# Attention scores of consecutive head pairs on the two diagonals of the matmul array, in two PSUM banks

## The chip, the cores and the metric

The program runs on one core of a Trainium2 chip. The metric is the device time of one execution in microseconds (us), the median of several executions. The matmul engine is called TensorE or PE; its weight loads are listed apart as PEld. VectorE is DVE, ScalarE is ACT, GpSimd is POOL, and SP is the engine whose queue issues the DMAs.

## The reference

A sliding-window attention (2 batches, 8 heads, 576 positions, head size 64, window 64) feeds two mixture blocks. In the attention stage, cut to what matters:

```python
scores = (1 / np.sqrt(64)) * np.matmul(q, k.transpose(0, 1, 3, 2))
rel = pos[:, None] - pos[None, :]
scores = np.where((rel >= 0) & (rel < 64), scores, -1e9)
attn = softmax(scores)                  # over the last axis, + 1e-9 in the divisor
x = np.matmul(attn, v)                  # then laid out as 1152 tokens x 512
```

Then `x` goes through four dense experts, `out += p_e * (relu(x @ w1[e]) @ w2[e])` (512 to 1024 to 512), and the sum of those through `g = prelu(out @ w_in); g @ w_out` (512 to 2048 to 512). Everything is float32.

## The kernel before

The attention is cut into 18 blocks `j` of 64 queries. A block looks at 128 keys, its own 64 and the 64 before. The eight heads are handled as four pairs `hp` (`NP = 4`), each pair with one head `h` on partitions 0 to 63 and the other on 64 to 127. For a block there are these steps:

- `S` (`att_S`): eight source matmuls, one for each head, contracting 64 partitions into 64 query rows by 128 keys (line 222). Head `h` reads partition half `h` of `q` and `k` and writes partition half `h` of one PSUM bank, so that all eight use one diagonal of the array: upper rows with left columns, lower rows with right columns. A float32 matmul appears in the trace as two MATMULs with a weight load each, so a block has 16. Then DVE adds the mask and takes the row extreme, once for each pair (line 233), and ACT takes the exponentials and their sums, once for each pair (line 236).
- `N` (`att_N`): DVE turns the sums into reciprocals (lines 242, 243), POOL multiplies (line 244).
- `PT` (`att_PT`): four transposes on TensorE (line 250), copied out by DVE or ACT (lines 254, 256).
- `PV` (`att_PV`): eight source matmuls (16 in the trace) over all 128 rows with 64 columns, the two heads of a pair on the two column halves (line 267). The result is split into a high and a low part (`xhi`, `xlo`; lines 272 to 278).

The order is written out by hand. For step `j` it is `PT(j-3)`, `N(j-1)`, `S(j)`, `PV(j-4)` (a little different at the start), with extras: `W` splits a quarter of the first weights (a DVE cast to `w1h`, line 157, and a POOL subtraction to `w1l`, line 158), and `Q` loads the next queries (line 90) and, once, the keys of the second batch (line 93). Blocks 0 to 9 come ahead of the dense layers; blocks 10 to 17 are spread between units of the first expert stage, one unit being 12 matmuls (`l1_unit`, line 290, or `l2_products`, line 324). After that TensorE runs dense units to the end. Each engine runs its instructions in the order written; SP's queue issues the DMAs in that order too, and a weight load (line 115, two buffers `ws`) waits until the splits of the load two before are done. The third weight load, `w2` of the first stage, is ahead of the small loads `praw` and `alph`, the fourth `q` load and the second `k` load in SP's queue.

PSUM is one pool of eight one-bank buffers, taken in turn. A tile of any kind is one such buffer.

Of the kernel before, what the change touches and what calls it, by code (L numbers as in the profile page):

```python
# [16 lines left out]
P = 128  # L17
# [8 lines left out]
def tile_kernel(ctx, tc, q, k, v, probs, w1, w2, w_in, w_out, alpha, out):  # L26
    nc = tc.nc


    B, H, D, S = k.shape  # L30
    NP = H // 2
    NT, DM = out.shape
    E, _, F = w1.shape
# [23 lines left out]
    def psum(name):  # L57
        return pp.tile([P, 512], F32, tag="ps", name=name)
# [154 lines left out]
    def att_S(j):  # L213
        g, jb = divmod(j, GB)
        m = mask0 if j % NB == 0 else mask
        ps = psum(f"s{j}")
        sv = ps.rearrange("p (a k) -> p a k", a=NP)

        for hp in range(NP):
            for h in range(2):  # L220
                r = slice(D * h, D * h + D)
                nc.tensor.matmul(  # L222
                    sv[r, hp, :],
                    lhsT=qs[g % 3][r, hp, jb * BLK:(jb + 1) * BLK],
                    rhs=kts[j // NB][r, hp, (j % NB) * BLK:(j % NB) * BLK + P],
                    start=True, stop=True, skip_group_check=True,
                )

        sm = ab.tile([P, NP, P], F32, tag="sm", bufs=2, name=f"sm{j}")
        st = ab.tile([P, 4, NP], F32, tag="st", bufs=4, name=f"st{j}")  # L230
        pt = ab.tile([P, NP, P], F32, tag="p", bufs=4, name=f"p{j}")
        for hp in range(NP):
            nc.vector.tensor_tensor_reduce(out=sm[:, hp, :], in0=sv[:, hp, :], in1=m, scale=-(D ** -0.5), scalar=3.0e38,  # L233
                                           op0=ALU.add, op1=ALU.min, accum_out=st[:, 0, hp:hp + 1])
        for hp in range(NP):
            nc.scalar.activation(out=pt[:, hp, :], in_=sm[:, hp, :], func=AF.Exp, scale=-1.0,  # L236
                                 bias=st[:, 0, hp:hp + 1], accum_out=st[:, 1, hp:hp + 1])
        p_t[j] = (pt, st)
# [20 lines left out]
    def att_PV(j):  # L259
        t, vt = pt_t.pop(j), v_t[j]  # L260
        ps = psum(f"pv{j}")[:, 0:NP * BLK]
        pv = ps.rearrange("p (a t) -> p a t", a=NP)

        for hp in range(NP):
            tv = t[:, hp, :].rearrange("p (h t) -> p h t", h=2)
            for h in range(2):
                nc.tensor.matmul(pv[64 * h:64 * h + 64, hp, :], lhsT=vt[:, 2 * hp + h, :], rhs=tv[:, h, :],  # L267
                                 start=True, stop=True, skip_group_check=True)
        c, o = divmod(j * BLK, CH)
        hi, lo = xhi[c][:, :, o:o + BLK], xlo[c][:, :, o:o + BLK]  # L270
        if o + BLK == CH:
            nc.scalar.activation(out=hi, in_=pv, func=AF.Copy)
            nc.vector.tensor_tensor(out=lo, in0=pv, in1=hi.bitcast(F32), op=ALU.subtract)
        else:
            xf = ab.tile([P, NP, BLK], F32, tag="xf", bufs=2, name=f"xf{j}")
            nc.vector.tensor_copy(out=xf, in_=pv)
            nc.gpsimd.tensor_copy(out=hi, in_=xf)
            nc.gpsimd.tensor_tensor(out=lo, in0=xf, in1=hi.bitcast(F32), op=ALU.subtract)
# [84 lines left out]
    with tc.manual_schedule():  # L363
# [24 lines left out]
        for j in range(NBLK + 4):  # L388
            last = (j - 3) % (CH // BLK) == 0
            pv = [("PV", j - 4)] if 0 <= j - 4 < NBLK else []  # L390
# [20 lines left out]
        def att_step():  # L411
            if pos[0] >= len(steps):
                return
            op, j = steps[pos[0]]
            pos[0] += 1
            if op == "Q":
                load_q(j)
                if j == 3:
                    load_k(1, 0, S)
            elif op == "S":  # L420
                att_S(j)
            elif op == "N":
                att_N(j)
            elif op == "W":
                split_w((1, 0, j // 2), j, fast=True)
            elif op == "PT":
                att_PT(j)
            else:
                att_PV(j)
                if j + 6 < NBLK:  # L430
                    load_v(j + 6)
                done[0] = j + 1
# [21 lines left out]
        s, c = NST - 1, NCH - 1  # L454
# [9 lines left out]
        a, b = S1 - 1, S1  # L464
# [7 lines left out]
        for s in range(1, NST):  # L472
            p = s - 1
# [27 lines left out]
        for i, unit in enumerate(order):  # L501
            op, s, c, a = unit
# [64 lines left out]
```

## Time and profile before

| what | us |
| --- | --- |
| three runs | 665.4, 667.4, 667.59 (median 667.4) |
| profiled execution, its own time | 667.37 |
| its span, first to last instruction | 665.6 |
| TensorE busy | 648.3 (97%) |
| mean granted TensorE clock | 0.995 |

The span is 1.8 us shorter than the time of the same execution. Busy time of TensorE counts each matmul from its start until its modelled end, so matmuls that overlap count once, and a busy engine need not be at its peak.

### The profile page before, as it was taken

Reading aid. Unit: us, or ns where it says so; the run is one execution under the profiler, and the core shown is the slowest. Engines: PE = TensorE matmul, PEld = TensorE weight load, DVE = VectorE, ACT = ScalarE, POOL = GpSimd, SP = SyncE. Lnnn points to the kernel's source line nnn. Section 1 sums busy time; section 2 is a strip of 40 time slices with the busy share of each in tenths; the row PEclk is TensorE's granted clock in tenths of the full one; section 3 lists DMA queues with packets and bytes.
Section 4 is the critical chain, followed back from the end, with each engine's and each line's share of the span. In section 5 each row is a group of like instructions: output and inputs, shape, how many; then the busy total and the mean of one; then the engine's idle time right before and its main releaser. Section 6 shows DMA issues by size and latency. Waiting matters only on the chain.

```text
span 665.6 us, 9448 instructions
## 1 busy us (share of the span) xinstructions
PE 648.3 (97%) x3720; PEld 584.6 (88%) x3720; DVE 390.4 (59%) x754; ACT 226.0 (34%) x539; POOL 187.7 (28%) x182
## 2 busy tenths in 40 slices
PE   5799999999999999999999999999999999999998
PEld 5598889999999999999999999999999887999897
DVE  3765543333383383393393342878777878888622
ACT  4554421221131131131131121334555443444331
POOL 5924410000030030030030000334665546566421
PEclk9999999999999999999999999999999998999999
DMA  8844011101121121121112101112111101110011
GB/s 292 252 139 129 1 64 64 63 1 64 63 64 63 64 64 63 64 64 64 64 64 63 64 1 63 64 64 64 41 61 61 57 37 64 64 64 0 32 40 71
DMA packets 25003, 45.71 MB, mean 69 GB/s; under 512 B 4352, under 2 KB 6656, under 8 KB 24960
## 3 DMA queue, kind: packets, MB, share of 16 engines
q1 hardware_dynamic: 24960, 45.12, 20.3%
q8 instruction: 29, 0.48, 0.3%
q14 instruction: 14, 0.11, 0.1%
HBM read 42.76 MB, written 2.36 MB: 68 GB/s over the span
## 4 chain that ended last, share of the span: by engine, by line
PE 94%; DVE 2%; DMA 2%; POOL 1%; issue 0%; SPq 0%; POOLq 0%; DVEq 0%
PE o L324 44%; PE h L290 44%; PE s L222 2%; DMA kt<-in_k_dram 2%; PE pt L250 1%; PE pv L267 1%; PE x L357 1%; POOL p L244 0%; POOL hl L317 0%; DVE sm L233 0%; DVE acc L349 0%; DVE gg L310 0%; POOL cy L197 0%; DVE cr L183 0%; POOL w1l L158 0%
## 5 line engine op out<-in xcount | busy, mean ns | idle before, releaser
L324 PE MATMUL o<-w2h,hl 128*128 128x512 f32 (+1 forms) x436 | 170.8, 392 | 1.3 <-POOL hl L317 1.3
L324 PE MATMUL o<-w2l,hh 128*128 128x512 f32 (+1 forms) x436 | 170.3, 390 | 0.1
L324 PE MATMUL o<-w2h,hh 128*128 128x512 f32 (+1 forms) x436 | 170.0, 390 | 0.0
L197 POOL TENSOR_TENSOR cy<-cy,ce 128x512 f32<-128x512 f32 x32 | 47.1, 1470 | 361.7 <-DVE ce L189 361.7
L300 ACT ACTIVATE hh<-h 128x384 fp32r<-128x384 f32 x96 | 47.2, 492 | 238.4 <-PE h L290 238.1
L290 PE MATMUL h<-xhi,w1l 128*128 128x384 f32 x576 | 125.5, 339 | 0.0
L290 PE MATMUL h<-xlo,w1h 128*128 128x384 f32 x576 | 123.4, 335 | 0.0
L290 PE MATMUL h<-xhi,w1h 128*128 128x384 f32 x576 | 123.0, 334 | 0.0
L301 DVE SCALAR_TENSOR_TENSOR hl<-h,hh 128x384 fp32r<-128x384 f32 x96 | 53.5, 557 | 106.1 <-ACT hh L300 106.1
L290 PEld LDWEIGHTS h<-xhi,w1l 128*128 128x128 f32 x576 | 102.1, 189 | 3.0 <-DVE st L242 0.2
L290 PEld LDWEIGHTS h<-xlo,w1h 128*128 128x128 f32 x576 | 102.8, 188 | 0.0
L290 PEld LDWEIGHTS h<-xhi,w1h 128*128 128x128 f32 x576 | 101.9, 188 | 0.0
L324 PEld LDWEIGHTS o<-w2h,hl 128*128 128x128 f32 x436 | 82.2, 188 | 20.4 <-POOL hl L317 3.4
L324 PEld LDWEIGHTS o<-w2l,hh 128*128 128x128 f32 x436 | 82.3, 189 | 16.3 <-ACT hh L316 0.5
L324 PEld LDWEIGHTS o<-w2h,hh 128*128 128x128 f32 x436 | 82.3, 189 | 16.1
L345 DVE SCALAR_TENSOR_TENSOR acc<-o,pn,acc 128x512 f32<-128x512 f32 x63 | 46.6, 748 | 73.6 <-PE o L324 73.6
L317 POOL TENSOR_TENSOR hl<-gg,hh 128x384 fp32r<-128x384 f32 x48 | 53.1, 1116 | 59.5 <-ACT hh L316 57.4
L310 DVE SCALAR_TENSOR_TENSOR gg<-rn,alph,gg 128x384 f32<-128x384 f32 x48 | 39.8, 830 | 34.9 <-ACT gg L309 34.7
L236 ACT ACTIVATE p<-sm,st 128x128 f32<-128x128 f32 x72 | 28.1, 391 | 28.4 <-DVE st L233 28.4
L308 ACT ACTIVATE rn<-h 128x384 f32<-128x384 f32 x48 | 23.3, 486 | 31.5 <-PE h L290 31.2
L316 ACT ACTIVATE hh<-gg 128x384 fp32r<-128x384 f32 x48 | 25.2, 524 | 16.8 <-DVE gg L310 16.8
L222 PE MATMUL s<-kt,q 64*64 64x128 f32 x288 | 22.4, 305 | 7.8 <-DMA kt<-in_k_dram 7.8
(64 smaller groups left out, 565.5 us busy)
## 6 DMA issues: line engine op xcount, KB each, us to landing
ws<-in_moe_w_dram SPq DMA_DIRECT2D x15, 1024.0 KB, 5.2
ws<-in_moe_w_in_dram SPq DMA_DIRECT2D x8, 1024.0 KB, 5.2
ws<-in_moe_w_out_dram SPq DMA_DIRECT2D x8, 1024.0 KB, 5.0
v<-in_v_dram SPq DMA_DIRECT2D x16, 256.0 KB, 7.3
q<-in_q_dram SPq DMA_DIRECT2D x6, 384.0 KB, 6.9
out_dram<-acc SPq DMA_DIRECT2D x8, 256.0 KB, 2.0
kt<-in_k_dram SPq DMA_DIRECT2D x1, 1152.0 KB, 7.7
ws<-in_moe_w_dram SPq DMA_DIRECT2D x2, 512.0 KB, 8.3
```

The source lines that it names most:

```text
L197: nc.gpsimd.tensor_tensor(out=y, in0=y, in1=e.bitcast(F32), op=ALU.mult)
L222: nc.tensor.matmul(sv[r, hp, :], lhsT=qs[g % 3][r, hp, jb * BLK:(jb + 1) * BLK], rhs=kts[j // NB][r, hp, (j % NB) * BLK:(j % NB) * BLK + P ...
L236: nc.scalar.activation(out=pt[:, hp, :], in_=sm[:, hp, :], func=AF.Exp, scale=-1.0, bias=st[:, 0, hp:hp + 1], accum_out=st[:, 1, hp:hp + 1])
L290: nc.tensor.matmul(ps, lhsT=w[:, d * P:(d + 1) * P], rhs=x[:, d, :], start=(n == 0), stop=(n == 3 * KD - 1))
L300: nc.scalar.activation(out=hh, in_=ps, func=AF.Relu)
L301: nc.vector.scalar_tensor_tensor(out=hl, in0=ps, scalar=0.0, in1=hh.bitcast(F32), op0=ALU.max, op1=ALU.subtract)
L308: nc.scalar.activation(out=rn, in_=ps, func=AF.Relu, scale=-1.0)
L310: nc.vector.scalar_tensor_tensor(out=gg, in0=rn, scalar=alph[:, col:col + 1], in1=gg, op0=ALU.mult, op1=ALU.add)
L316: nc.scalar.activation(out=hh_, in_=gg_, func=AF.Copy)
L317: nc.gpsimd.tensor_tensor(out=hl_, in0=gg_, in1=hh_.bitcast(F32), op=ALU.subtract)
L324: nc.tensor.matmul(ps, lhsT=h_t[s, c, f][a][:, t * P:(t + 1) * P], rhs=w_t[2, s, f][b][:, cols], start=(n == 0), stop=(n == 3 * NF - 1))
L345: nc.vector.scalar_tensor_tensor(out=at, in0=ps, scalar=sc, in1=at, op0=ALU.mult, op1=ALU.add)
```

## The change

Pairs with an odd number swap the halves of the output: head 0 (upper rows) writes partitions 64 to 127, head 1 (lower rows) writes 0 to 63. They thus use the other diagonal of the array. The even pairs' scores stand in one PSUM tile, the odd pairs' in a second one, each of which is half filled. In `att_PV` the halves are read back accordingly. The number of matmuls, of DVE, ACT and POOL instructions, and of DMAs stays as it was.

```diff
     def att_S(j):
         g, jb = divmod(j, GB)
         m = mask0 if j % NB == 0 else mask
-        ps = psum(f"s{j}")
-        sv = ps.rearrange("p (a k) -> p a k", a=NP)
+
+        ps = [psum(f"s{j}_{i}")[:, 0:NP // 2 * P].rearrange("p (a k) -> p a k", k=P) for i in range(2)]
+        sv = [ps[hp % 2][:, hp // 2, :] for hp in range(NP)]
 
         for hp in range(NP):
             for h in range(2):
-                r = slice(D * h, D * h + D)
+                r, c = [slice(D * x, D * x + D) for x in (h, h ^ hp & 1)]
                 nc.tensor.matmul(
-                    sv[r, hp, :],
+                    sv[hp][c],
                     lhsT=qs[g % 3][r, hp, jb * BLK:(jb + 1) * BLK],
...
-            nc.vector.tensor_tensor_reduce(out=sm[:, hp, :], in0=sv[:, hp, :], in1=m, scale=-(D ** -0.5), scalar=3.0e38,
+            nc.vector.tensor_tensor_reduce(out=sm[:, hp, :], in0=sv[hp], in1=m, scale=-(D ** -0.5), scalar=3.0e38,
...
-                nc.tensor.matmul(pv[64 * h:64 * h + 64, hp, :], lhsT=vt[:, 2 * hp + h, :], rhs=tv[:, h, :],
+                nc.tensor.matmul(pv[64 * h:64 * h + 64, hp, :], lhsT=vt[:, 2 * hp + h, :], rhs=tv[:, h ^ hp & 1, :],
```

## Rows read from the trace of the kernel before

**Rows 1.** The page: busy time, and by slice TensorE's granted clock and DMA.

```profile
PE 648.3 (97%) x3720; PEld 584.6 (88%) x3720; DVE 390.4 (59%) x754; ACT 226.0 (34%) x539; POOL 187.7 (28%) x182
...
PE 94%; DVE 2%; DMA 2%; POOL 1%; issue 0%; SPq 0%; POOLq 0%; DVEq 0%
```

**Rows 2.** The chain that ended last, 36 to 95 us: start, length, what.

```profile
38.67 1.02 PE s L222 x16
39.69 0.61 PE pv L267 x16
40.30 0.59 PE pt L250 x4
40.89 2.09 PE h L290 x12
...
64.64 4.17 PE h L290 x24
```

**Rows 3.** Line 222, 33 to 80 us: durations in ns (min/median/max), starts.

```profile
L222 PEld LDWEIGHTS s<-kt,q x128: 129/133/133, 38.6 to 73.8; 64*64 64x64 f32 x128
L222 PE MATMUL s<-kt,q x128: 269/269/320, 38.6 to 74.0; 64*64 64x128 f32 x128
```

**Rows 4.** Line 222 in a tenth-us stretch: width, busy (instructions in flight), clock, DMA.

```profile
39.08:39.19 0.11, 0.11 (x6) 0.11 (x4) 1.00 0.05 19
```

**Rows 5.** The chain, 0 to 36 us.

```profile
5.83 3.69 PE s L222 x32
...
23.43 7.68 DMA kt<-in_k_dram
...
31.24 1.74 PE s L222 x16
32.98 1.04 PE pt L250 x4
```

**Rows 6.** The chain over the whole span, at the first dense units.

```profile
34.02 4.65 PE h L290 x24
```

**Rows 7.** DVE in order of time, 5 to 40 us.

```profile
7.97 0.29 DVE L233 CUSTOM_DVE_ANT_0 sm<-s,mask 128x128 f32<-128x128 f32 x1 [6.83 <-PE s L222]
...
12.38 0.40 DVE L157 CAST w1h<-ws 128x512 fp32r<-128x512 f32 x1
13.86 0.29 DVE L233 CUSTOM_DVE_ANT_0 sm<-s,mask 128x128 f32<-128x128 f32 x1 [1.08 <-PE s L222]
```

**Rows 8.** ACT in order of time, 8.3 to 13.6 us.

```profile
8.30 0.40 ACT L236 ACTIVATE p<-sm,st 128x128 f32<-128x128 f32 x1 [6.28 <-DVE st L233]
...
13.12 0.57 ACT L256 ACTIVATE ptr<-pt 128x512 f32<-128x512 f32 x1
```

**Rows 9.** POOL in order of time, 11 to 24 us.

```profile
11.04 1.04 POOL L244 TENSOR_TENSOR p<-p,st 128x512 f32<-128x512 f32 x1 [6.30 <-DVE st L243]
12.61 1.07 POOL L244 TENSOR_TENSOR p<-p,st 128x512 f32<-128x512 f32 x1 [0.53 <-DVE st L243]
13.63 1.27 POOL L158 TENSOR_TENSOR w1l<-ws,w1h 128x512 fp32r<-128x512 f32 x1
15.28 1.06 POOL L244 TENSOR_TENSOR p<-p,st 128x512 f32<-128x512 f32 x1 [0.38 <-DVE st L243]
16.31 1.27 POOL L158 TENSOR_TENSOR w1l<-ws,w1h 128x512 fp32r<-128x512 f32 x1
```

**Rows 10.** SP's queue in order of time.

```profile
17.61 0.38 SPq L115 DMA_DIRECT2D ws<-in_moe_w_dram  x1
```

**Rows 11.** The first weight load's landing after its issue at 3.90 us.

```profile
DMA to landing us min/median/max: 7.8/7.8/7.8
```

**Rows 12.** One stretch: width, busy PE, PEld, DVE, ACT, POOL, clock, DMA share, GB/s.

```profile
16.00:18.00 2.00, 1.63 (x22) 1.27 (x20) 1.97 (x13) 1.14 (x6) 2.00 (x3) 1.00 0.01 5
```

**Rows 13.** Stretches around the stop before 31 us, same columns.

```profile
28.10:31.50 3.40, 1.41 (x25) 1.13 (x27) 1.85 (x11) 2.39 (x10) 3.24 (x6) 1.00 1.05 404
31.60:34.90 3.30, 3.30 (x22) 2.97 (x19) 1.83 (x11) 1.49 (x8) 1.04 (x1) 0.50 1.05 327
```

## Prediction

> **What bounds the kernel now.** I read the page first: TensorE is busy 97% of the span and carries 94% of the chain that ended last [rows 1]. A change on TensorE can therefore count in full, but only where TensorE itself sets the pace. For that I read the chain in order of time. From 34 us on it is TensorE work almost without a break: a block's scores take 1.02 us on it, its values 0.61, its transposes 0.59, then 12 dense matmuls 2.09 [rows 2]. Eight of the 18 score blocks lie there: 128 MATMULs of line 222 between 38.6 and 74.0 us, 16 a block [rows 3]. Before 34 us the chain is mixed: scores, POOL, DVE, and a key load that is issued at 23.43 us and holds up block 9 until 31.24 us [rows 5].
>
> Next, what a block's 1.02 us is made of. Transposes and scores both stream 128 float32 columns. The transposes use the whole array one after the other: four in 0.59 us. Were the 16 scores also one after the other, they would need four times that less some start-up, at least 1.8 us. Say one slot is t and filling and draining the array cost D: 4t + D = 0.59 and 8t + D = 1.02 give t = 0.108 and D = 0.16 us. The value matmuls stream half as many columns: 8 x 0.054 + 0.16 = 0.59, against 0.61 in the row. So the trace says that two matmuls already run side by side in a slot, in the scores on the two quarters of one diagonal, in the values on the two column halves over all rows. The other diagonal lies idle during the scores.
>
> **The change, part by part.** The 16 MATMULs of a block stay, and so do all DVE, ACT, POOL and DMA instructions. Only the place of half of them in the array moves.
>
> Scores on the dense part of the chain. With four quarters at work a block has four slots: 4 x 0.108 + 0.16 = 0.59 us, 0.43 less than 1.02. What no row shows is two row halves writing the same 64 output partitions at once. The nearest rows bound it: the values show two column halves reading the same partitions together (gain as above); if the new pairing does not overlap at all, a block keeps eight slots (gain 0). In between, if the second diagonal starts one slot late, there are five slots and a gain of 0.32. I take 0.43, since nothing in the rows separates the two diagonals but the output partitions, and those now lie in two banks. Eight blocks: 3.44 us. TensorE waits for nothing else in this stretch, so I count it in full.
>
> Block 9 starts when the key load lands and takes 1.74 us, as its clock falls to half on the way [rows 5, 13]. It gains 0.43 at full and 0.85 at half clock. I take 0.6.
>
> The start. Blocks 0 and 1 take 3.69 us for 16 slots, 0.23 a slot, twice the later ones [rows 5]. DVE gets block 0 at 7.97 us [rows 7]. Four slots fewer bring that to 7.05, and ACT's first exponential from 8.30 to 7.4. ACT runs three blocks without a gap until 13.12, 1.61 each [rows 8]; it now ends them at 9.0, 10.6 and 12.2. Block 1's normalization no longer stands behind block 2's scores, and POOL's multiply goes from 12.61 to about 11.2 [rows 9], ending at 12.3. DVE's first weight cast at 12.38 [rows 7] may move to 11.75, as its load, issued at 3.90, has landed at 11.70 [rows 11]. POOL's first subtraction goes from 13.63 to 12.3, and DVE's row extremes of block 3 from 13.86 to 12.2, right behind the cast (TensorE has block 3 by then: POOL's first multiply at 9.7 instead of 11.04, transposes, four slots). POOL's third multiply then follows at 13.7 instead of 15.28 and its second subtraction at 14.8 instead of 16.31 [rows 7, 9]. That subtraction frees the buffer for the third weight load, which SP issues at 17.61 [rows 10]; now at about 16.1. Behind it in SP's queue stand the small loads, a query load and the key load. The DMA engines are idle in front of it, share 0.01 from 16 to 18 us [rows 12], so the whole train can move forward, and the key load lands about 1.5 us sooner, with block 9. Bounds: 0, if the train runs into the loads before it or the key load is held up on its way anyway, and 1.6. I take 1.4.
>
> PSUM. A block takes two buffers of the eight instead of one, so five instead of four are taken per step of about 4.3 us, and a buffer comes round after 1.6 steps, 7 us, instead of 2. Copies out follow within about 2 us, so this costs nothing; without that cover the first score matmul would wait for DVE. DVE can start a pair as soon as its bank is done, no later than now. Cost 0; upper bound one more wait instruction a block on TensorE's queue, below 0.05 us each, 0.4 over eight blocks.
>
> Here one rule speaks against the change. In the row, weight loads and matmuls of both row halves are in flight at any moment: in 0.11 us, six matmuls and four loads, both busy throughout [rows 4]. The Trainium skill, "TensorE: Matmul & The Clock Gate", Part 3 (what overlaps and what doesn't), says that a weight load overlaps matmuls in flight only when its row group differs. By that rule the present block could not load at all under its matmuls, so the trace disagrees, and the sum goes by the row.
>
> Sum: 3.44 + 0.6 + 1.4 = 5.4 us. The profiled execution took 667.37 us (span 665.6), as the median, 667.4. Its time becomes 662.0 us, its span 660.2.
>
> **The rivals.**
>
> *The start's gain is swallowed.* The key load takes 7.68 us from issue to landing [rows 5], with other loads beside it; if it lands as before, block 9 waits for it as before, and only 3.44 + 0.6 are left: 663.4 us. For it speaks the load's length, against it the idle DMA engines in front.
>
> *The diagonals don't overlap.* Two row halves on the same output partitions may take turns. Then a block keeps eight slots and nothing else changes: 667.4 us. The trace neither shows nor excludes this. A sentence on the page alone: the Trainium skill, "TensorEngine Tiling (Array Packing)", Gotcha 1, lets different row tiles work at once when they write different banks, which would give the four slots.
>
> *Slower: the weight loads come into the open.* If a load into one diagonal can't run while the other diagonal's matmuls hold the same rows, each of the four pairs of a block begins with its load, 0.133 us [rows 3], in front: 0.53 a block on top of eight slots. Eight blocks 4.3, block 9 0.5, and blocks 0 and 1 at half clock 8 x 0.23 = 1.8: 6.6 us, 674.0. It decides from 0.107 us a pair, where it eats the 0.43. Against it speaks rows 4, where loads run under matmuls of the same rows already; but there a quarter loads only for itself. The rule of the Trainium skill named above would give this case.
>
> *The clock.* After a stretch where TensorE was busy 1.41 of 3.40 us, the granted clock was 0.50, that is 1.2 of 2.4 GHz, for 31.6 to 34.9 us [rows 13]. It cost 0.72 in block 9, 0.45 in its transposes and 0.48 in the first 24 dense matmuls (4.65 against 4.17), 1.65 in all [rows 2, 5, 6]. Shorter scores leave TensorE idle longer in the start; the fall may come earlier and be over before block 9, or come once more. This is 1.65 either way and shifts each case.
>
> **How the numbers follow.** Four slots with the start's gain 0.55 (662.0), four or five slots without it 0.20 (663.4), no overlap 0.15 (667.4), loads in the open 0.10 (674.0). Own range of the first two: lowest 667.4 - (1.6 + 0.85 + 3.5 + 1.65) = 659.8; highest without the start's gain, with 0.43 for block 9, 3.0 for the others and a fall of the clock more, 667.4 - 1.8 = 665.6. That holds three in four; to eight in ten the range must reach the no-overlap case: 659.8 to 667.6. A measurement of this kernel can tell about 0.3%, 2.0 us, from no change. Faster by more 0.75, within 0.15, slower 0.10.
>
> **What would show it.** Right: line 222's 16 MATMULs in 0.59 us from block to next operation, eight matmuls or more in flight in a tenth of a us, the third weight load issued near 16.1 and block 9 started near 29.8 us, and everything from 90 us on shifted by one amount. Wrong: a block still at 1.02 us (no overlap) or above 1.1 (loads); block 9 still at 31.2 us (start swallowed); stops of TensorE on DVE in front of the scores (PSUM buffers); a second stretch at half clock.

## The result, and the profile after

The changed kernel takes 660.4 us (median of six runs, 660.15 to 663.17), the kernel before, on the same chip, 667.28 (665.4 to 667.59). The ratio is 0.991, with a 95% interval of 0.989 to 0.993. The forecast was 662.0.

The profiled execution took 660.32 us, its span is 658.5 against 665.6 before, so there are 7.1 us to find. The page of the changed kernel gives TensorE, with the same 3720 MATMULs, 8.4 us less busy time than [rows 1], and 92% of the chain instead of 94:

```profile
PE 639.9 (97%) x3720; PEld 574.3 (87%) x3720; DVE 390.7 (59%) x754; ACT 224.9 (34%) x539; POOL 187.9 (29%) x182
...
PE 92%; DVE 4%; DMA 2%; POOL 2%; issue 1%; ACT 0%; SPq 0%; POOLq 0%; DVEq 0%
```

The chain of the changed kernel, 36 to 95 us (start, length, what), answers to [rows 2]:

```profile
42.69 0.60 PE s L223 x16
43.28 0.61 PE pv L268 x16
43.90 0.59 PE pt L251 x4
...
66.47 0.60 PE s L223 x16
67.07 2.31 PE h L291 x12
```

A block of scores has gone from 1.02 to 0.60 us, and nothing around it has changed. The last block's successor, 12 dense matmuls, starts at 67.07 us. Before, it started at 74.22:

```profile
74.22 2.31 PE h L290 x12
```

The 7.15 us between them are the 7.1 of the span: the whole gain is made by then, and none is lost behind it.

The stretches of a tenth of a us inside one block, for line 223 alone (width, PE and PEld busy with the instructions in flight, clock, DMA), answer to [rows 4]:

```profile
38.73:38.84 0.11, 0.11 (x4) 0.11 (x8) 1.00 0.05 19
38.84:38.95 0.11, 0.11 (x8) 0.11 (x12) 1.00 0.18 37
38.95:39.06 0.11, 0.11 (x12) 0.11 (x8) 1.00 0.10 37
39.06:39.17 0.11, 0.11 (x14) 0.10 (x4) 1.00 0.14 37
```

And line 223 from 33 to 80 us (durations in ns as min/median/max, first and last start), as [rows 3]:

```profile
L223 PEld LDWEIGHTS s<-kt,q x128: 129/133/133, 34.8 to 66.7; 64*64 64x64 f32 x128
L223 PE MATMUL s<-kt,q x128: 269/269/320, 34.8 to 66.8; 64*64 64x128 f32 x128
```

Each instruction takes as long as before. The 16 matmuls of a block start in four groups, 0, 160, 269 and 378 ns after the first, where before there were eight groups of two. In place of six matmuls and four loads, up to 14 matmuls and up to 12 loads stand in one such stretch, and in the middle two at least eight of each. The gain is overlap and nothing else.

The chain of the changed kernel from 0 to 36 us, as [rows 5] and, in its last row, [rows 6]:

```profile
12.14 1.06 PE s L223 x16
...
17.09 0.60 PE s L223 x16
...
23.31 6.04 DMA kt<-in_k_dram
...
29.48 0.67 PE s L223 x16
30.15 0.59 PE pt L251 x4
30.74 4.18 PE h L291 x24
```

The key load is issued only 0.12 us sooner than before, but takes 6.04 us instead of 7.68, and block 9 begins at 29.48 instead of 31.24. From there on TensorE runs at full clock, where before it fell to half. The stretches around (width; busy PE, PEld, DVE, ACT, POOL; clock, DMA share, GB/s) show it, as [rows 13]:

```profile
28.10:31.50 3.40, 2.42 (x40) 2.14 (x37) 1.81 (x11) 2.04 (x11) 2.94 (x6) 1.00 1.04 397
31.60:34.90 3.30, 3.30 (x24) 3.05 (x23) 2.72 (x9) 2.41 (x10) 1.80 (x2) 1.00 1.04 336
```

So the 7.1 us of the span fall into these parts:

| part | before | after | gain |
| --- | --- | --- | --- |
| block 9 begins | 31.24 | 29.48 | 1.76 |
| block 9 | 1.74 | 0.67 | 1.07 |
| its transposes | 1.04 | 0.59 | 0.45 |
| first 24 dense matmuls | 4.65 | 4.18 | 0.47 |
| eight blocks in the dense part | 1.02 each | 0.60 each | 3.38 |
| sum | | | 7.13 |

### The profile page after: what moved, and what is told of

It reads as the page before. It is cut to its first block, busy times and chain, and to the rows that moved or that the text cites. A ratio compares the mean times of both kernels' runs of the same rounds, so it can differ in the third digit from the quotient of the medians.

```text
span 658.5 us, 9458 instructions
## 1 busy us (share of the span) xinstructions
PE 639.9 (97%) x3720; PEld 574.3 (87%) x3720; DVE 390.7 (59%) x754; ACT 224.9 (34%) x539; POOL 187.9 (29%) x182
## 4 chain that ended last, share of the span: by engine, by line
PE 92%; DVE 4%; DMA 2%; POOL 2%; issue 1%; ACT 0%; SPq 0%; POOLq 0%; DVEq 0%
PE o L325 43%; PE h L291 43%; DMA kt<-in_k_dram 2%; PE s L223 2%; PE pt L251 2%; PE pv L268 1%; DVE gg L311 1%; PE x L358 1%; POOL hl L318 1%; DVE ca L179 1%; DVE cr L183 0%; DVE ca L178 0%; DVE acc L350 0%; POOL p L245 0%; DVE w2l L205 0%
## 5 line engine op out<-in xcount | busy, mean ns | idle before, releaser
L325 PEld LDWEIGHTS o<-w2l,hh 128*128 128x128 f32 x436 | 81.9, 188 | 16.1 <-ACT hh L317 0.5
L179 DVE TENSOR_SCALAR ca<-ca 128x512 f32<-128x512 f32 x32 | 28.9, 904 | 1.1
```

The costliest lines, as they stand in the source:

```text
L179: nc.vector.tensor_scalar(out=a.bitcast(F32), in0=a.bitcast(F32), scalar1=LOW, scalar2=HIGH, op0=ALU.max, op1=ALU.min)
L325: nc.tensor.matmul(ps, lhsT=h_t[s, c, f][a][:, t * P:(t + 1) * P], rhs=w_t[2, s, f][b][:, cols], start=(n == 0), stop=(n == 3 * NF - 1))
```

## The experiments

Each ratio is taken against runs of the kernel before on the same chip. The first four, a second four and the last three had a chip each, on which the kernel before took 667.05, 667.06 and 665.9 us (medians of 24, 18 and 11 runs).

**Both diagonals in the dense part alone** (blocks 10 to 17).

```diff
-                r, c = [slice(D * x, D * x + D) for x in (h, h ^ hp & 1)]
+                r, c = [slice(D * x, D * x + D) for x in (h, h ^ (hp & 1 if j >= 10 else 0))]
```

PSUM tiles and line 268 follow the same condition.

> Only blocks 10 to 17, those between dense units, use both diagonals and two banks; blocks 0 to 9 stay as before. Theory A (a shorter block counts in full where TensorE sets the pace): these eight blocks take 0.60 us each instead of 1.02, block 9 starts near 31.2 us as before, and the time is 667.3 - 8 x 0.42 = 663.9 us. Rival B (the gain comes from the start and the clock; what the dense blocks save is lost again on DVE or in PSUM buffers): 666 us or more. Rival C (the key load's landing and the clock are luck of the execution): 663.9 or, with the clock staying full, 662.3, whatever the start does.

It took 664.03 us (seven runs), ratio 0.9956 (0.9934 to 0.9979). Its chain from 20 to 48 us (the scores are line 227 here):

```profile
23.29 7.97 DMA kt<-in_k_dram
...
31.39 1.09 PE s L227 x16
...
37.25 0.60 PE s L227 x16
```

The dense blocks have their 0.60, and the start is that of the kernel before: long key load, block 9 at 31.39 us. By medians this part is worth 3.0 us, by its blocks 8 x 0.42 = 3.4. The profiled execution, 662.57 us, is one of the shorter of the seven (661.74 to 665.25): its clock did not fall behind the key load.

**Both diagonals in the start alone** (blocks 0 to 9): the same edit with `j < 10`.

> Only blocks 0 to 9 use both diagonals; blocks 10 to 17 stay as before. Theory A (start and clock follow from the shorter scores of the first blocks): block 9 starts near 29.5 us, takes 0.6 us at full clock, and the first dense unit starts near 30.7 us; gain 1.76 + 1.07 + 0.92 = 3.75, time 663.5 us. Rival C (landing of the key load and clock are luck, nothing of the change): block 9 near 31.2 us, only its own 0.43 to 0.85 us gained, 666.6 us.

It took 664.25 us (twelve runs), ratio 0.9964 (0.9948 to 0.998). Its chain, same stretch:

```profile
23.22 6.22 DMA kt<-in_k_dram
...
29.57 0.67 PE s L227 x16
...
35.00 1.02 PE s L227 x16
```

Block 9 comes early here, at 29.57 us, with the short key load, and the dense blocks stay at 1.02. By medians 2.8 us; the two halves add up to 5.8 us, and the whole change gave 6.9 in one measurement and 5.6 in another (below), with intervals of 1.1 to 1.6 us either way.

**Two banks, one diagonal.** The scores stand in two PSUM tiles as in the change, but every pair uses the diagonal of before.

```diff
-                r, c = [slice(D * x, D * x + D) for x in (h, h ^ hp & 1)]
+                r, c = [slice(D * x, D * x + D) for x in (h, h)]
...
-                nc.tensor.matmul(pv[64 * h:64 * h + 64, hp, :], lhsT=vt[:, 2 * hp + h, :], rhs=tv[:, h ^ hp & 1, :],
+                nc.tensor.matmul(pv[64 * h:64 * h + 64, hp, :], lhsT=vt[:, 2 * hp + h, :], rhs=tv[:, h, :],
```

> Two banks as in the change, but all pairs stay on the one diagonal. Theory A (the second diagonal makes the gain): a block takes 1.02 us as before, 667.3 us. Rival D (the second bank makes it, since DVE may start on a finished bank or matmuls to one bank hinder each other): blocks near 0.6 us or DVE's row extremes earlier, below 665 us. Rival E (two buffers a block cost something): above 668.5 us.

It took 664.88 us (median of ten runs, seven of them between 663.93 and 665.47, three at 667.26 or more), ratio 0.9984 (0.9964 to 1.0005): not told from the kernel before. Its chain:

```profile
23.01 6.10 DMA kt<-in_k_dram
...
29.24 1.09 PE s L223 x16
...
39.42 1.02 PE s L223 x16
```

The second bank by itself shortens no block: 1.02 us. Yet this profile, too, has the short key load and block 9 at 29.24 us. A key load that lands early thus doesn't need the second diagonal. The counterpart, both diagonals in one bank, was not tried, so no run shows whether the gain needs the second bank.

**Another order of the pairs.** Here two pairs of the same diagonal follow each other, so that TensorE finds the other diagonal's matmuls only behind eight in the queue.

```diff
-        for hp in range(NP):
+        for hp in (0, 2, 1, 3):
             for h in range(2):
```

> The change, with the pairs issued in the order 0, 2, 1, 3, so that each diagonal's two pairs come one after the other: eight MATMULs for one diagonal, then eight for the other. Theory F (TensorE looks far enough ahead for the other diagonal's matmuls to pass those that wait): four slots, 0.60 us a block, 660.4 us. Rival G (a quarter takes only one waiting matmul, and those behind it stop all others): the second diagonal starts three slots late, seven slots, 0.92 us a block, eight blocks 2.6 us longer and the start too: 664 to 666 us.

It took 662.47 us (four runs, 659.94 to 663.29), ratio 0.9931 (0.9904 to 0.9957). Its chain:

```profile
22.69 7.99 DMA kt<-in_k_dram
...
30.82 1.15 PE s L223 x16
31.96 1.04 PE pt L251 x4
...
41.70 0.61 PE s L223 x16
```

The blocks take 0.61 us, so the order of the pairs hardly matters, and theory F holds: matmuls of the other diagonal start although eight of the first stand in front of them. The trace shows it too. Two MATMULs of a block carry the signal that a bank is done. The first bank's is the eighth as the program writes them, but it starts as the 14th of 16, 385 ns after the first; six that are written behind it have started by then. In this execution the key load was a long one, and the clock fell behind it as it did before the change: 1.15, 1.04 us. That, and not the blocks, sets this execution (663.29 us) 3 us behind the change; the lowest of its four runs is at the change's level.

**The keys sooner.** In the change, and in the kernel before, the small loads `praw` and `alph` go behind the second key load in SP's queue.

```diff
-        nc.sync.dma_start(out=praw, in_=probs.rearrange("(t p) e -> p t e", p=P))
-        nc.sync.dma_start(out=alph, in_=alpha.rearrange("(c p) -> p c", p=P))
...
                 if j == 3:
                     load_k(1, 0, S)
+                    nc.sync.dma_start(out=praw, in_=probs.rearrange("(t p) e -> p t e", p=P))
+                    nc.sync.dma_start(out=alph, in_=alpha.rearrange("(c p) -> p c", p=P))
```

> The change, with the two small loads of many short packets (probabilities and alpha) issued behind the second key load instead of in front of it. Theory A2 (block 9 waits for the key load, whose place behind the small loads and whose landing vary from one execution to the next): the key load is issued near 19 us instead of 23.3 and has landed by 27 us; block 9 follows the value matmuls ahead of it without a wait, near 28.4 instead of 29.5 us, 1.0 us less where the keys came early (659.4 us) and more where they came late, so the runs lie closer together. Rival H (something else, POOL or DVE, holds block 9 as much): block 9 stays near 29.5 us, 660.4 us.

> The kernel before, with the same two loads moved behind the key load. Theory A2: block 9 near 29.3 instead of 31.2 us, no stop of two us in front of it, so the clock does not fall to half there: 1.9 us in each run and 1.65 more in the runs where the clock fell, 664 us; what the change then still gives, this against the change with the same move, is about 4.5 us. Rival H: 667 us.

The change with it took 660.04 us (six runs), ratio 0.9906 (0.9886 to 0.9927); the kernel before with it 664.09 (twelve runs), ratio 0.9962 (0.9949 to 0.9976). SP's queue in the former, in order of time:

```profile
16.93 0.38 SPq L115 DMA_DIRECT2D ws<-in_moe_w_dram  x1
17.35 1.79 SPq L90 DMA_DIRECT2D q<-in_q_dram  x1
19.18 0.43 SPq L93 DMA_DIRECT2D kt<-in_k_dram  x1
```

The key load is issued 4 us sooner and no longer stands on the chain of either kernel. The difference of the two, 4.05 us, is then what the two diagonals are worth where the landing of the keys plays no part: 8 x 0.42 = 3.4 in the dense part, and some 0.6 ahead of it (with early keys the dense matmuls start at 30.49 us in the change and at 31.05 in the kernel before). The changed kernel hardly gains from the early keys, because POOL comes next: block 9 starts at 28.44 us, as theory A2 had it, but its transposes wait for POOL. The end of its chain in front of the dense matmuls:

```profile
28.79 1.01 POOL p L245
...
29.84 0.65 PE pt L251 x4
30.49 4.24 PE h L291 x24
```

The dense matmuls start at 30.49 instead of 30.74 us.

**A warm TensorE.** Ten matmuls (20 in the trace) of a zeroed 128 x 128 tile ahead of block 0, into a PSUM tile of their own that nobody reads; in the change alone, and with the early keys.

```diff
+        nc.vector.memset(zero, 0.0)
+        for _ in range(10):
+            nc.tensor.matmul(wps[:, 0:P], lhsT=zero, rhs=zero, start=True, stop=True)
         load_q(0)
```

> The change, with ten matmuls of a zeroed tile on TensorE in front of block 0, results unused, while the first loads are under way. Theory I (the start was shortened less than forecast since TensorE stayed at half clock until 16.6 us, where the kernel before had full clock from 11 us): block 0 and the transposes up to 16 us run at full clock, the third weight load is issued near 16.0 instead of 16.9 us and the key load 0.9 us sooner: 659.5 us. Rival J (the key load's landing hangs on the loads around it and not on its issue): third weight load sooner, block 9 as before, 660.4 us. Zeroes may not raise the clock; then nothing moves.

> Both: small loads behind the key load, and the ten matmuls in front of block 0. Theory I with A2: nothing waits for keys, and the start is 0.9 us shorter than with the moved loads alone: 658.5 us. Rival J: as the moved loads alone, 659.4 us.

The first took 662.8 us (seven runs, two of them at 659.68 and 660.41), ratio 0.9938 (0.9915 to 0.9961), so it gains nothing over the change. Its chain:

```profile
1.06 4.63 PE warm L369 x20
...
10.56 1.11 PE pt L253 x4
...
22.21 8.72 DMA kt<-in_k_dram
...
31.06 1.13 PE s L225 x16
```

The transposes at 10.56 us are no faster than in the change without them (1.12 at 11.03). The granted clock tells why (columns as in [rows 12]):

```profile
7.20:10.50 3.30, 0.68 (x24) 0.44 (x17) 2.69 (x27) 3.25 (x17) 1.03 (x1) 1.00 1.05 375
10.60:13.90 3.30, 3.30 (x28) 2.31 (x32) 2.48 (x13) 2.65 (x14) 2.31 (x2) 0.50 1.08 375
```

The trace's record of the clock begins with 1.00 at 7.16 us, so the matmuls on zeros did bring full clock early. But TensorE then waited 2.68 us for POOL, and from 10.57 to 13.98 us the clock was at 0.50. So the start stayed slow, and what a clock held up through the start would be worth is not shown. The key load was issued 1.1 us sooner than in the change and took 8.72 us: of the eight profiles with this order of loads, the one that issued it first has the longest landing. With the early keys as well, the time is 659.72 (six runs, 659.62 to 659.99), ratio 0.9903 (0.9881 to 0.9925), the lowest of all and nearer to rival J's 659.4 than to theory I's 658.5, but the 0.6 to 0.7 us to the change lie within the intervals. Here, too, the clock was at 0.50 again, from 9.38 to 16.21 us.

**The change again**, unedited, on the chip of the last two runs below.

> The change itself, once more, for its own spread and a second trace. Theory A2 (the key load lands early or late from one execution to the next, whatever the scores take; late goes with a stop of TensorE and a fall of its clock): two groups of runs, near 660.3 and near 663 us. Theory A (the shorter scores themselves bring the keys early): all runs near 660.4 us, block 9 at 29.5 us again.

It took 660.32 us (six runs, 659.85 to 661.04), ratio 0.9906 (0.9881 to 0.993). Its key load took 6.35 us from 22.65, block 9 began at 29.13, and the clock stayed up behind it. All six lie near 660.4, as theory A has it. But the other order of the pairs and the warm TensorE, which have the same two diagonals, had the long key load in their profiles, so shorter scores alone do not bring the keys early. Of the change's twelve runs, eleven lie between 659.85 and 661.04, one at 663.17.

**POOL relieved.** With the early keys, two or all four subtractions of the first weights go from POOL to DVE.

```diff
-                nc.gpsimd.tensor_tensor(out=lv, in0=src, in1=hv.bitcast(F32), op=ALU.subtract)
+                (nc.vector if f > 1 else nc.gpsimd).tensor_tensor(out=lv, in0=src, in1=hv.bitcast(F32), op=ALU.subtract)
```

> The change, the small loads behind the key load, and the last two of the four low parts of the first weights computed on DVE instead of POOL. Theory K (once the keys are early, POOL sets the pace of the start: it is busy without a gap from 15 to 26 us): POOL has 2 x 1.27 us less to do, DVE 2 x 0.69 more, block 9 near 27 instead of 28.4 us, 658.7 us. Rival L (DVE then is late by as much, as it stands in front of the row extremes): 660 us.

> As the one before, with all four low parts on DVE. Theory K: the third weight load's buffer is free about 0.6 us sooner as well, POOL has 5.1 us less in all, block 9 near 26 us, 658 us. Rival L: DVE, with 2.8 us more in front of the row extremes, holds the start; 659 us or more.

They took 661.9 and 661.8 us (six runs each), ratios 0.9931 (0.9908 to 0.9955) and 0.9929 (0.9906 to 0.9951), above the 0.9906 of the early keys alone. The chain of the first, before its dense matmuls:

```profile
26.30 1.66 ACT p L237 x8
27.98 0.96 DVE st L243
...
30.11 0.96 ACT p L237 x5
...
31.96 4.40 PE h L291 x24
```

DVE and ACT take POOL's place on it, and the dense matmuls start at 31.96 us, 1.5 later than with the early keys alone. So the gain of theory K did not come. Rival L's account, DVE late, fits, but its 660 us was too low. In that execution TensorE's clock was also at 0.50, from 23.11 to 29.94 us, but TensorE is not on the chain there.

## Why the prediction was right, and where it was not

**Dense scores: right.** Forecast 0.59 us a block and 3.44 in all, measured 0.60 and 3.38. The reckoning from transposes and values (slots of 0.108 us, 0.16 for filling and draining) holds with four slots; the groups of starts lie 109 ns apart behind the first. The rival that the diagonals don't overlap falls with it. Each bank of the change is still written by both row halves, on different partitions, as the one bank before was, where the trace starts two such matmuls 7 ns apart; row halves did not need a bank each for that.

**Loads in the open: refuted.** At 0.60 us a block nothing is left of four loads of 0.133 in front. Eight and more loads stand beside as many matmuls, which run in the same rows through both diagonals. The rule of the Trainium skill, "TensorE: Matmul & The Clock Gate", Part 3 (what overlaps and what doesn't), that a load overlaps only matmuls of another row group, disagrees with this trace as it did with the one before.

**PSUM and waits: right.** The chain shows no stop of TensorE on DVE in front of scores, and the second bank alone (1.02 us a block) costs nothing.

**The start: the gain came, but not by the step that was to bring it.** Forecast: third weight load at 16.1 us, key load 1.5 us sooner. SP's queue in the changed kernel:

```profile
16.93 0.38 SPq L115 DMA_DIRECT2D ws<-in_moe_w_dram  x1
...
19.30 3.96 SPq L90 DMA_DIRECT2D q<-in_q_dram  x1
23.31 0.43 SPq L93 DMA_DIRECT2D kt<-in_k_dram  x1
```

Two steps failed. First, the weight load came 0.68 us sooner than in [rows 10] and not 1.5. DVE did get block 0 at 7.38 us, against 7.97 in [rows 7]. But it waited for the weights until 12.07 to cast them and for block 3 until 13.24, where the forecast had 12.2:

```profile
7.38 0.29 DVE L234 CUSTOM_DVE_ANT_0 sm<-s,mask 128x128 f32<-128x128 f32 x1 [6.24 <-PE s L223]
...
12.07 0.71 DVE L157 CAST w1h<-ws 128x512 fp32r<-128x512 f32 x1 [0.75 <-DMA ws<-in_moe_w_dram]
13.24 0.29 DVE L234 CUSTOM_DVE_ANT_0 sm<-s,mask 128x128 f32<-128x128 f32 x1 [0.46 <-PE s L223]
```

Block 3 was late because TensorE, which had gone through the first three blocks in 2.84 us instead of 5.36, still took 1.12 us for the transposes at 11.03 and 1.06 for the scores at 12.14, near twice the 0.66 and 0.60 of later ones. The trace's record of the granted clock begins with 1.00 at 16.63 us in the changed kernel and at 11.05 before; for the time ahead of that there is no record. The four profiles with one diagonal in the start have it begin between 9.96 and 11.05 us, the five with two there, and the work of TensorE and DVE otherwise as it was, between 13.77 and 17.17. Before, TensorE had worked on the first three blocks without a break for 5.36 us, and its transposes at 12.13 already took 0.66. The forecast took the later, shorter durations for block 3; shorter blocks ahead of it came with a later rise of the clock, which the prediction did not price.

Second, "the whole train can move forward" came to 0.12 us only: the query load in front of the keys stays in SP's queue until 23.26 us, against 23.38 before, though the weight load ahead of it came 0.68 us sooner. Its 3.96 us are 4.07 before. The profile puts 3.8 us of them down to a wait for TensorE. But the buffer that this load fills was last read by block 2, whose scores end at 8.94 us, so a wait for TensorE does not explain it. The record points at the small loads. With these behind the keys the entry takes only 1.79 us, and the long ones are theirs and those behind them: 3.43 us for `alph`, 5.20 for three `v` loads. A stretch in which the DMA engines are busy but move little has moved back with them. It lies at 22 to 24 us in the change (first row) and at 26 to 28 us in the change with the early keys (second row; columns as in [rows 12]):

```profile
22.00:24.00 2.00, 1.58 (x36) 1.11 (x34) 1.25 (x10) 1.82 (x9) 1.92 (x4) 1.00 0.84 31
...
26.00:28.00 2.00, 1.72 (x40) 1.24 (x32) 1.97 (x10) 0.51 (x3) 1.92 (x4) 1.00 0.96 38
```

In the first stretch 2359 of 2373 packets are under 512 bytes, in the second 2439 of 2461. That the query load's entry waits for these packets is likely from this, but not shown by itself.

So the rival "the start's gain is swallowed" was right about the issue, and would have been right about the time had the key load taken its 7.68 us. It took 6.04. With the loads in this order it has two lengths:

| kernel | issued | to landing | TensorE's stop before block 9 | clock after it |
| --- | --- | --- | --- | --- |
| before | 23.43 | 7.68 | 1.99 | falls |
| dense part alone | 23.29 | 7.97 | 2.21 | stays |
| other order | 22.69 | 7.99 | 2.26 | falls |
| warm TensorE | 22.21 | 8.72 | 3.01 | falls |
| change | 23.31 | 6.04 | 0.98 | stays |
| change again | 22.65 | 6.35 | 1.00 | stays |
| start alone | 23.22 | 6.22 | 1.43 | stays |
| two banks | 23.01 | 6.10 | 0.33 | stays |

All times are us; the stop is TensorE's idle time ended by the key load. The length follows neither the time of issue nor the number of diagonals. What decides it stays open; that it hangs on what else is being loaded is argued, not shown. That the changed kernel has the short one in nearly all of its runs is likely from their times (eleven of twelve within 1.2 us), but only two of them have a trace.

**Block 9 and the clock: the size was off.** The forecast gave block 9 0.6, as between its gain at full and at half clock, and left the clock as it was. Block 9 itself gained 1.07: some 0.42 from its slots (1.09 us in the dense-part kernel, at full clock, against 0.67), the rest because the clock didn't fall. The transposes and dense matmuls behind it gave 0.92 more. The granted clock rows show 0.50, half of 2.4 GHz, behind stops of 1.99, 2.26 and 3.01 us, and no fall behind 0.33 to 1.43; behind the 2.21 of the dense-part kernel it stayed up, so the stop alone does not decide. The clock was named as a rival, 1.65 us either way; it came in on the good side, and 662.0 - 1.65 = 660.35 is what was measured. That the sum meets so closely is luck: the start gave 0.36 more than its term, and block 9 with the clock 0.26 less than 0.6 + 1.65.

In sum: 3.38 for 3.44, 1.76 for 1.4, 1.07 for 0.6 and 0.92 for nothing. Of the 6.9 us between the medians, about 4 are the diagonals' own, as the two kernels with early keys show. The rest is a key load that landed sooner, and the clock that this spared. How large this rest is hangs on the executions too: the kernel before, unchanged, took between 664.24 and 669.27 us in its 53 runs on the three chips, 25 of them at 666.42 or less and 28 at 666.88 or more.

## What to carry to other kernels

Matmuls of 64 rows by 64 columns have four places in the array, and scores of head pairs with head size 64 fill only two when each head writes the half that it reads, as here; swapping the output halves of every other pair, in a bank of its own, cost no matmul and no work on another engine and took 41% off each block (1.02 to 0.60 us). How many matmuls run side by side can be read before the change by comparing one group with another that streams as many columns through the whole array. Where such a step stands behind a load, price the load's landing and what TensorE's clock does behind the stop as cases of their own: here they were some 3 of 7 us. Moving two small loads out of the way brought the runs together, to 659.36 to 660.53 us for the change and 663.86 to 664.78 for the kernel before.

## What the runs showed of the hardware

- The order of the pairs did not matter (0.61 against 0.60 us): TensorE starts matmuls of the other diagonal although eight of the first stand in front, and starts the eighth as the 14th.
- The same key load takes 6.04 to 8.72 us from its issue, in kernels whose loads are the same and in the same order.
- Loads of 18 and 8 KB in packets under 512 bytes went with two us in which the DMA engines were busy for 0.84 of the time and moved 31 GB/s; between 20 and 22 us it was 314.
- In the first 16 us of the changed kernel TensorE's instructions take nearly twice their later time. The record of the granted clock begins only at 16.63 us, and a stretch without a record is printed as 1.00. At the start, durations tell more than that column.
- 4.63 us of matmuls on zeros ahead of block 0 brought the granted clock to 1.00 by 7.16 us. After TensorE's wait of 2.68 us it was at 0.50 from 10.57 on, and the transposes took 1.11 us, as without the zeros (1.12).
